# Zero rows as tasks of the sync queue, row numbers loaded per query block, and a new order, in a block-sparse attention with an MLP on one Trainium2 core

## The chip, the cores and the metric

One core of a Trainium2 chip runs the whole program: TensorE (PE), VectorE (DVE), ScalarE (ACT), GpSimd (POOL), the sync engine (SP) that only issues transfers here, and 16 DMA engines. The metric is device microseconds of one execution. The kernel before takes 737.58 us, the median of 3 runs (735.38 to 740.02).

## The reference

`q`, `k`, `v` have 4 batches, 8 heads, 768 positions and 64 columns. Positions fall into 24 blocks of 32. A query block sees its own and the two neighbouring key blocks, the first and the last block, and three sampled ones; the first and the last query block see all keys.

```python
    scores = scale * np.matmul(q, k.transpose(0, 1, 3, 2))
    mask = np.abs(blk_i - blk_j) <= window
    mask = mask | (blk_i == 0) | (blk_j == 0) | (blk_i == n_blocks - 1) | (blk_j == n_blocks - 1)
    for qb in range(n_blocks):
        for kb in sampled_blocks[qb]:
            mask[qb * block:(qb + 1) * block, kb * block:(kb + 1) * block] = True
    ...
    return np.matmul(attn, v)
    ...
    h = x @ w_in                      # 3072 x 512 by 512 x 2048
    g = h * np.tanh(softplus(h))
    return g @ w_out                  # 2048 x 512
```

## The kernel before, in words

**Attention.** Each batch is 13 jobs (52 in all): the two full query blocks alone, the other 22 in pairs. A job is: scores `s` on TensorE, row maximum `mx` (DVE) and its scaled form `nb`, exponentials `pt` (ACT), a transpose of the probabilities, the product `o` with the values, division `xs` and a 32 x 32 transpose `tx` (DVE), and the split of the result into two f16 parts `xh` and `xl`. Batch 0 works in f32 and transposes on TensorE (`t`, then a copy `pp`); batches 1 to 3 work in f16 pairs and transpose by a DMA of the sync queue (`pp_dma`, L880). There is one scores buffer in PSUM, so the scores of a job wait for the exponentials of the job before it.

**Keys and values of a pair.** `gather_k` copies three sampled key blocks into the buffer `kg` (POOL, or ACT when the planner likes that better); `gather_v` issues four or five DMAs on the sync queue from a copy of the values in DRAM, `vd`, into `vg`. Where a sampled block is already in the window or is sampled twice, the row number points at 32 **zero rows** behind the values of `vd`. `which` works out the row numbers (`offk`, `offv`) from the sampled blocks with some twenty small DVE instructions, clears a piece of SBUF and stores it as the zero rows of the four batches, four DMAs on ACT's queue (L400). The row numbers come into an engine's registers by `values_load` in `blocks_at` (TENSOR_LOAD, L663): six numbers at a time, those of both blocks of a pair, once for each engine that gathers for the pair.

**The MLP.** `w_in` comes in 8 pieces of 1 MB (`wr`, three buffers), `w_out` in 16 (`wor`). They are float64 in pairs of int32: DVE decodes them (L1040, L1043, L1046), a gram product on TensorE and two small steps give a scale, and ACT, POOL and DVE split them into two f16 parts `wi` and `wo`. For each of 12 tiles of 256 positions: 16 units of `h` (12 products each, L1184), the activation `g` on ACT, DVE and POOL, and 16 units of `y` (6 products each, L1244). The first `h` needs the result of jobs 0 to 4 and the first piece of `wi`.

**What sets the order.** The kernel writes all its tasks into a planner (`Plan`) that runs when the program is built. It keeps an estimated time for each engine, takes the task that can start first, and breaks ties by the numbers of `PRIO`. `START` holds an earliest time for the scores of the first 18 jobs, and `RES` how much MLP work is to be left when the last scores start. Each engine gets its instructions in the order in which they were taken and waits in that order. Where the planner expects TensorE idle in the first 150 us, `emit` puts products of zeros there (L1019). Each DMA takes the next of eight completion semaphores, in the order of the program, so a DMA waits until the one eight places ahead of it has landed.

Of the kernel before, what the change touches and what calls it, by code (L numbers as in the profile page):

```python
# [10 lines left out]
F16 = mybir.dt.float16  # L11
# [19 lines left out]
PRIO = {  # L31
    "zeros": (-1475,),
    "load32 k": (-845.8,),
    "load32 q": (-521.8, -448.8, -133.8),
    "load v": (-335.4, -495, -187.9, 230.7),
    "which": (-366.4,),
    "globals": (-1100, -6.6, -629.2, -149.6),
# [16 lines left out]
    "gsc": (-489.7,),  # L54
    "open": (507.5,),
    "s": (-363.8, 257.2, 138.7, 739),
    "mx": (-244, -319.1, 454.4, -635.3),
    "nb": (91.8, 609.2, 401.3, -77.9),
    "ex": (879.3, 387.6, 575.9, -27.9),
    "t": (-67.7, 16),  # L60
    "pp": (-8.1,),
    "o": (249.5, -772.8, 56.2, 280.6),
    "xs": (164.1, 687.9, 486.7, -162.2),
    "tx": (-80.3, 357.3, -117, -301.3),
    "xh": (795.7, -92.6, 151.3, -180.3),
    "xl": (-108.8, -149.4, -464.4, 487.1),
    "gather k": (-91.6, -283.6, -211.3, -794.3),
    "gather v": (-465, -812.9, -151.1, -1036),
    "load wo": (-701.2, -485, -180.9, 187.3),
    "decode wor": (338.6, 334.9, 656.5, 297.7),  # L70
    "gram y": (620.2,),
    "diag y": (-604.3,),
    "rootp wo": (-372.6,),
    "root wo": (-947.3,),
    "wo t": (112.9, -511.6, 53.8, 551.6),
    "wo hi": (-369.6, -312.8, -250.1, -464.2),
    "wo lo": (129.2, -136.8, -300.6, -232.5),
    "load k": (59, 59, 59, -132.3),
    "ss k": (70, 70, 70, 131),
    "sc k": (4, 356.4, -47.2, -105.6),  # L80
    "rootp k": (60, -634.9, -788.4, -43.6),
    "root k": (7, -763, -202.2, 176.7),
    "hi k": (52, 298, 502.1, 134.5),
    "lo k": (-79, -308.4, -18.8, -82.9),
    "load q": (59, 59, 59, 922.3),
    "ss q": (70, 70, 70, -319.9),
    "rootp q": (60, 231.2, 189.5, 65.7),
    "root q": (7, -0.7, 482.1, -278.2),
    "hi q": (52, -617.7, -813.9, -431.7),
    "lo q": (-79, -301.9, -459.2, 220.5),  # L90
    "clear": (-871.6,),
    "dense v": (-524.8, -820.3, -116.4, -411.5),
    "sc v": (4, -451.1, 413.1, -242.8),
    "ends": (13, 1272, 408.6, 260.5),
    "hi v": (52, 429.3, 414.7, 163.6),
    "lo v": (-79, -46.1, -130.6, -361.2),
    "hsc": (-629.6, -765.4, -588.2, 494.6),
    "osc": (-86, 750, 394.5, 691.1),
    "h16": (17, -34.8, 37, -408.3),
    "l16": (-40, -538.2, -718.8, -730.1),  # L100
    "tdma": (-60, 514.2, -156.5, 135.9),
    "xc": (1, 324.4, -257.5, 928.6),
    "kw": (8, -141.1, 764, 224.6),
    "hs": (268.3, -203.1, 55.1, 458.3),
    "us": (-570.1, -103.3, -302.2, -862.9),
    "us1": (240.2, -236.2, 174.8, 321.8),
    "us2": (515.7, 236.1, -874.1, -128.7),
    "ln": (-41.8, 181.7, -203.2, -276.7),
    "un": (353.1, 608.6, 449.1, 52.3),
    "hm": (-273.3, -620.2, 41, -1033),  # L110
    "gh": (-571.7, 417.5, -81.6, 428.6),
    "gl": (-58.7, 25.1, -179.3, -85.7),
    "ys": (-505.2, -22.3, -674.9, -34.6),
    "out": (577.4, 504.7, -100.7, -419.3),
# [21 lines left out]
class Plan:  # L136
# [47 lines left out]
    def emit(self, pace):  # L184
# [16 lines left out]
        while todo:  # L201
# [34 lines left out]
            if t.eng == "PE" and self.zeros and self.FROM < start < self.TILL and idle > 0.25:  # L236
                self.zeros(int(idle / 0.22))
            for e in t.ways:
# [43 lines left out]
def attn_mish_kernel(ctx: ExitStack, tc: tile.TileContext, qT, kT, v, sampled, blocks, w_in, w_out, out):  # L282
# [74 lines left out]
    def which(new):  # L357
        room = new(sb, "raw", ("z",), [P, RAW])
        at = [H * VW // 2]
# [28 lines left out]
        for r in range(1, NR):  # L388
            for r2 in range(r):
# [284 lines left out]
    def gather_k(su):  # L674
# [3 lines left out]
        def fn(eng):  # L678
            for j, c0 in zip(blocks_at(mybir.EngineType.Pool if eng == "POOL" else mybir.EngineType.Activation,
# [5 lines left out]
                else:  # L685
                    nc.scalar.activation(out=dst, in_=src, func=AF.Copy)  # L686
        add("POOL", 0.75 if exact(b) else 1.05, lambda: fn("POOL"), r=KT3(b) + ["off"], w=[("kg", n)], use=[("kt", b)], port=2, key=K("gather k", b),
            also=[("ACT", 0.65 if exact(b) else 0.95, lambda: fn("ACT"))])
        if su["whole"]:
            add("DVE", 0.44, lambda: nc.vector.tensor_copy(  # L690
                out=kgs[n][:, :, 0:WK], in_=tl["kt", b][:, :, (qb - 1) * BS:(qb + 2) * BS]),
                r=KT3(b), w=[("kw", n)], use=[("kt", b)], port=True, key=K("kw", b))

    def gather_v(su):
# [6 lines left out]
        def fn():  # L701
# [59 lines left out]
    def attend(job):  # L761
# [121 lines left out]
        for j in range(nt):  # L883
            kj, kpp, kp16 = ("t", i, j), ("pp", i, j), ("p16", i, j)
            if exact(b):
# [95 lines left out]
        add("DVE", 0.45 if nsu > 1 else 0.3, tx_fn, r=[("xs", i)], w=[("tx", i)], new=[("tx", ("tx", i))], key=K("tx", b))  # L981

# [19 lines left out]
        def xl_fn(eng):  # L1002
            run(lambda x, hi, lo: (nc.vector if eng == "DVE" else nc.gpsimd).tensor_tensor(out=lo, in0=x, in1=hi, op=ALU.subtract))  # L1003
# [459 lines left out]
```

## Time and profile before

| | us |
|---|---|
| median of 3 runs | 737.58 (735.38 to 740.02) |
| profiled execution, device time | 731.8 |
| its span, first to last instruction | 729.7 |
| around the span | 2.1 |
| TensorE busy | 687.9, of which products of zeros 39.1 |
| DVE, ACT, POOL busy | 565.8, 546.9, 241.7 |

Busy time says how long an engine worked, not what it waited for. Loading registers and issuing DMAs is not counted as busy, so that an engine of the profile can look idle while its sequencer is held. TensorE's busy time has work that produces nothing in it, the products of zeros.

### The profile page before, as it was taken

How to read it: one execution, taken by the hardware profiler on the slowest of the kernel's cores; microseconds unless marked ns; L12 is line 12 of the kernel's file. 1: busy time of each engine (PE TensorE's matmuls, PEld its weight loads, DVE VectorE, ACT ScalarE, POOL GpSimd, SP SyncE). 2: the span in 40 equal slices, each digit the busy share in tenths (PEclk: the TensorE clock that was granted, in tenths of full speed). 3: DMA queues.
4: the chain of work that ended last, by engine and by line, in shares of the span. 5: the costliest groups of instructions: out<-in, count | busy, mean ns of one | idle time of the engine just before them, and what ended most of it. 6: DMA issues, size and time to landing. Idle time of an engine off the chain costs nothing.

```text
span 729.7 us, 25410 instructions
## 1 busy us (share of the span) xinstructions
PE 687.9 (94%) x10383; PEld 452.4 (62%) x10383; DVE 565.8 (78%) x1065; ACT 546.9 (75%) x908; POOL 241.7 (33%) x314
## 2 busy tenths in 40 slices
PE   9888888898899899899999999999999999999997
PEld 3545576774466666565666666666666667666653
DVE  3788789899988878999888887979889878454350
ACT  2666666999888877898978889988898976464550
POOL 2266432276424423331423223543536521100000
PEclk9999999999999999999999999999999999999999
DMA  7978698432767877857798986795786666500000
GB/s 264 362 215 245 209 281 223 133 84 86 195 125 172 163 181 200 183 132 225 137 189 139 210 195 138 188 213 132 148 170 149 150 129 169 133 15 15 15 16 30
DMA packets 144600, 115.95 MB, mean 159 GB/s; under 512 B 96739, under 2 KB 107492, under 8 KB 144484
## 3 DMA queue, kind: packets, MB, share of 16 engines
q1 hardware_dynamic: 144288, 114.06, 62.9%
q8 instruction: 82, 1.34, 0.8%
q14 instruction: 34, 0.28, 0.1%
q10 hardware_dynamic: 196, 0.27, 0.1%
HBM read 79.32 MB, written 12.95 MB: 126 GB/s over the span
## 4 chain that ended last, share of the span: by engine, by line
PE 41%; DVE 16%; ACT 15%; DMA 13%; issue 7%; POOL 4%; SPq 2%; ACTq 2%; POOLq 1%; DVEq 0%
PE y L1244 18%; PE h L1184 16%; DMA raw_q<-in_q_dram 4%; ACT pt L825 3%; DMA pp<-p 2%; DMA wr<-in_moe_w_in_dram 2%; PE o L926 2%; DVE mx L799 2%; PE s L756 2%; ACT us L1215 2%; ACT us L1216 2%; DVE p L876 2%; DMA wor<-in_moe_w_out_dram 2%; ACTq L663 1%; DVE hs L1217 1%
## 5 line engine op out<-in xcount | busy, mean ns | idle before, releaser
L1184 PE MATMUL h<-xh,wi 128*128 128x256 f16 x1536 | 284.0, 274 | 1.3 <-POOL xh L1000 1.1
L1244 PE MATMUL y<-wo,g 128*128 128x512 f16 x1152 | 277.9, 380 | 4.6 <-ACT ys L1255 2.9
L1184 PEld LDWEIGHTS <-wi 128*128 128x128 f16 x2304 | 222.0, 98 | 60.4 <-issue 8.4
L1184 PE MATMUL h<-xl,wi 128*128 128x256 f16 x768 | 209.9, 273 | 0.9 <-POOL xl L1003 0.9
L1244 PEld LDWEIGHTS <-g 128*128 128x128 f16 x1152 | 109.7, 98 | 110.9 <-issue 11.4
L684 POOL COPY kg<-kt 128x256 f16 (+1 forms) x138 | 69.4, 542 | 149.4 <-PE s L756 110.2
L825 ACT ACTIVATE pt<-s,nb,ns 128x256 f32<-128x256 f32 (+1 forms) x208 | 106.6, 578 | 5.9 <-DVE nb L814 5.1
L1193 ACT ACTIVATE hs<-h,gsc 128x512 f32<-128x512 f32 x96 | 65.1, 678 | 44.8 <-PE h L1184 44.8
L1217 DVE SCALAR_TENSOR_TENSOR hs<-us,hs 128x1024 f32<-128x1024 f32 x48 | 59.9, 1249 | 23.5 <-ACT us L1216 23.2
L876 DVE SCALAR_TENSOR_TENSOR p<-pt,p 128x512 f16<-128x512 f32 (+1 forms) x102 | 65.5, 665 | 5.8 <-ACT p L869 5.1
L686 ACT ACTIVATE kg<-kt 128x256 f16 (+1 forms) x126 | 38.6, 373 | 30.6 <-DVE v L628 9.8
L799 DVE TENSOR_REDUCE mx<-s 128x4 f32<-128x1024 f32 x44 | 53.4, 1213 | 10.1 <-PE s L756 7.2
L1000 POOL CAST xh<-tx 128x256 f16<-128x256 f32 (+1 forms) x35 | 22.8, 659 | 114.0 <-DVE tx L980 102.4
L1211 DVE TENSOR_SCALAR us<-us 128x1024 f32<-128x1024 f32 x48 | 35.0, 729 | 30.1 <-ACT us L1207 29.7
L1003 POOL TENSOR_TENSOR xl<-tx,xh 128x256 f16<-128x256 f32 (+1 forms) x53 | 43.0, 816 | 42.1 <-ACT xh L998 23.5
L1207 ACT ACTIVATE us<-hs,hsc 128x1024 f32<-128x1024 f32 x48 | 55.1, 1148 | 1.0
L1215 ACT ACTIVATE us<-us 128x1024 f32<-128x1024 f32 x48 | 50.6, 1055 | 5.5 <-POOL us L1213 4.7
L1214 ACT ACTIVATE us<-us 128x1024 f32<-128x1024 f32 x37 | 39.1, 1056 | 18.4 <-DVE us L1211 18.3
L1216 ACT ACTIVATE us<-us 128x1024 f32<-128x1024 f32 x48 | 50.5, 1054 | 0.8
L1228 POOL TENSOR_TENSOR g<-hs,g 128x1024 f16<-128x1024 f32 x16 | 38.0, 2375 | 34.5 <-DVE g L1225 18.7
L1019 PE MATMUL zeros<-z 128*128 128x512 f16 x153 | 39.1, 402 | 3.7 <-issue 2.1
L926 PEld LDWEIGHTS <-pp 128*32 128x32 f16 x2952 | 32.6, 97 | 13.7 <-issue 11.4
(205 smaller groups left out, 908.7 us busy)
## 6 DMA issues: line engine op xcount, KB each, us to landing
vg<-vd SPq DMA_DIRECT2D x304, 65.0 KB, 2.3
vg<-vd SPq DMA_DIRECT2D x80, 195.0 KB, 3.1
wr<-in_moe_w_in_dram SPq DMA_DIRECT2D x8, 1024.0 KB, 9.2
wor<-in_moe_w_out_dram SPq DMA_DIRECT2D x16, 512.0 KB, 5.2
vd<-v SPq DMA_DIRECT2D x12, 520.0 KB, 5.0
raw_v<-in_v_dram SPq DMA_DIRECT2D x12, 512.0 KB, 6.1
out_dram<-ys SPq DMA_DIRECT2D x24, 256.0 KB, 2.3
raw_k<-in_k_dram SPq DMA_DIRECT2D x9, 512.0 KB, 5.9
```

What stands on the lines that cost most here:

```text
L684: nc.gpsimd.tensor_copy(out=dst, in_=src)
L799: nc.vector.tensor_reduce(out=mx.rearrange("p g w -> p (g w)"), in_=tl[ks].rearrange("p g (w k) -> p (g w) k", k=KT), axis=AX.X, op=ALU.max)
L825: ex = lambda o, x, g, w: nc.scalar.activation(out=o, in_=x, func=AF.Exp, bias=nb[:, g, w:w + 1], scale=ns(w)[:, 0:1])
L876: nc.vector.scalar_tensor_tensor(out=x[:, 1, cs], in0=src, scalar=PSC, in1=x[:, 0, cs], op0=ALU.mult, op1=ALU.subtract)
L926: nc.tensor.matmul(o[cs, at] if v1 == VW else o[cs, at, 0:v1 - v0], p[:, k, g, cs], x, start=j == 0 and g == 0 and k == 0 and n == 0, stop ...
L1184: nc.tensor.matmul(h[:, f2].rearrange("p (s q) -> p s q", q=BS), wi[:, fp, w, cc, fs], x[:, :, cc], start=f2 == 0 and k == 0, stop=f2 == 1 ...
L1193: nc.scalar.activation(out=tl[kq][:, 2 * (fp % 2):2 * (fp % 2) + 2], in_=tl[kh], func=AF.Copy, scale=gsc[:, fp:fp + 1])
L1207: nc.scalar.activation(out=new(sb, "us", ku, [P, 4, TT]), in_=hs(), func=AF.Exp, scale=hsc[:, b:b + 1])
L1215: add("ACT", 0.97, lambda: nc.scalar.activation(out=us(), in_=us(), func=AF.Ln, bias=1.0), w=[ku], key=K("ln", b))
L1216: add("ACT", 0.97, lambda: nc.scalar.activation(out=us(), in_=us(), func=AF.Exp, scale=-1.0), w=[ku], key=K("un", b))
L1217: add("DVE", 1.15, lambda: nc.vector.scalar_tensor_tensor(out=hs(), in0=us(), scalar=-0.5, in1=hs(), op0=ALU.add, op1=ALU.mult), r=[ku], w ...
L1244: nc.tensor.matmul(tl[ky], tl["g", b, t, k][:, g, f, q], wo[:, fc, w], start=fc == 0 and n == 0, stop=fc == NFC - 1 and n == 2)
```

## The change

- `which` no longer stores the zero rows. The cleared piece stays as `tl["z"]`, in a buffer of the ring `hs` in place of `raw`, and a task `zrow` for each batch stores it from the sync queue. `gather_v` of a batch waits for its own batch's zero rows.
- `su["first"]` is the query block itself and `n = NR`: three row numbers are loaded for each query block, on the engine that gathers for it.
- The number of products of zeros for an idle stretch is `(idle - 0.3) / 0.25` (0.4 in the first 15 us) in place of `idle / 0.22`: 105 are left of 153.
- Some of the planner's durations are other ones, and all of `PRIO`, `RES` and `START`, so that the order is another one on every engine.

```diff
 PRIO = {
-    "zeros": (-1475,),
...
+    "zrow": (-213.9, 259.7, 665, 36.4),
+    "zeros": (-1718,),
...
@@ emit
-                self.zeros(int(idle / 0.22))
+                self.zeros(int((idle - 0.3) / (0.25 if start > 15.0 else 0.4)))
@@ which
-        room = new(sb, "raw", ("z",), [P, RAW])
+        room = new(sb, "hs", ("z",), [P, 4, TT]).rearrange("p c t -> p (c t)")
...
-        z = room[0:BS, 0:H * VW // 2]
-        nc.gpsimd.memset(z, 0.0)
-        for b in range(B):
-            nc.scalar.dma_start(out=vd[b][S:S + BS].rearrange("s h d -> s (h d)"), in_=z if exact(b) else z.bitcast(F16))
+        tl["z"] = room[0:BS, 0:H * VW // 2]
+        nc.gpsimd.memset(tl["z"], 0.0)
+
+    def zrow(b):
+        nc.sync.dma_start(out=vd[b][S:S + BS].rearrange("s h d -> s (h d)"), in_=tl["z"] if exact(b) else tl["z"].bitcast(F16))
@@ blocks_at
-            n = 2 * NR
+            n = NR
@@ planner's durations
-        add("POOL", 0.75 if exact(b) else 1.05, lambda: fn("POOL"), ...
-            also=[("ACT", 0.65 if exact(b) else 0.95, lambda: fn("ACT"))])
+        add("POOL", 1.0 if exact(b) else 1.3, lambda: fn("POOL"), ...
+            also=[("ACT", 0.85 if exact(b) else 1.15, lambda: fn("ACT"))])
-        add("SP", 2.7, fn, r=VD3(b) + ["off", "z"], w=[("vg", n)], ...
+        add("SP", 3.1, fn, r=VD3(b) + ["off", ("z", b)], w=[("vg", n)], ...
-            add("SP", 0.3, lambda j=j: pp_dma(j), ...
+            add("SP", 1.35, lambda j=j: pp_dma(j), ...
-        add("DVE", 0.45 if nsu > 1 else 0.3, tx_fn, ...
+        add("DVE", 0.6 if nsu > 1 else 0.4, tx_fn, ...
@@ jobs
-            su["first"] = job["sus"][0]["qb"]
+            su["first"] = su["qb"]
@@ tasks
+    for b in range(B):
+        add("SP", 0.45, lambda b=b: zrow(b), r=["z"], w=[("z", b)], use=[("z",)], key=K("zrow", b), lat=2.2, kind=("dma", 0.4, 1))
@@ pace
-    RES, START = 142.9, [0, 2.2, 0.9, 28.4, 939.4, 56.8, 14.9, 34.5, 18.6, 102, ...
+    RES, START = 134.7, [5.3, 0, 0, 8.3, 31.4, 57, 38.1, 69.3, 35.4, 462.6, ...
```

The sync queue at the start of the program, before (`kt` and `q` are keys and queries of batch 0, `raw_v` its values, `wr` pieces of `w_in`, `vd` the values in DRAM):

```order
L512 DMA kt_0_123<-in_k_dram 128x4x768
L512 DMA q_0_0_157<-in_q_dram 128x4x256
L530 DMA raw_v_0_1_161<-in_v_dram 128x2x512
L512 DMA q_0_1_163<-in_q_dram 128x4x256
L530 DMA raw_v_0_0_165<-in_v_dram 128x2x512
L530 DMA raw_v_0_2_167<-in_v_dram 128x2x512
L1032 DMA wr_0_169<-in_moe_w_in_dram 128x4x512
L1032 DMA wr_1_171<-in_moe_w_in_dram 128x4x512
L1032 DMA wr_2_173<-in_moe_w_in_dram 128x4x512
```

The same place in the changed kernel:

```order
L514 DMA q_0_1_123<-in_q_dram 128x4x256
L514 DMA q_0_0_153<-in_q_dram 128x4x256
L514 DMA kt_0_157<-in_k_dram 128x4x768
L532 DMA raw_v_0_1_159<-in_v_dram 128x2x512
L532 DMA raw_v_0_0_161<-in_v_dram 128x2x512
L1034 DMA wr_0_163<-in_moe_w_in_dram 128x4x512
L532 DMA raw_v_0_2_165<-in_v_dram 128x2x512
L1034 DMA wr_1_167<-in_moe_w_in_dram 128x4x512
L402 DMA vd0_60<-z_125 32x520
L402 DMA vd3_63<-z_125 32x1040
L402 DMA vd1_61<-z_125 32x1040
L1034 DMA wr_2_215<-in_moe_w_in_dram 128x4x512
```

The first piece of `w_in` stands one place earlier, and the four zero stores, which stood on ACT's queue ahead of two of the value loads, stand behind the second piece.

VectorE around the scale of the last pieces of `w_in` (`gsc`), before (`xs_4`, `tx_4`: the result of job 4; `mx_7`: the maximum of job 7's scores; `wor`: pieces of `w_out`):

```order
L1154 TENSOR_SCALAR gsc_76<-iv_i_73,rg_1421 128x8
L1159 TENSOR_SCALAR hsc_81<-gmx_77,iv_x_78 128x1
L1043 SCALAR_TENSOR_TENSOR wo_72<-wor_4_1219,wo_72 128x512
L1046 SCALAR_TENSOR_TENSOR wo_72<-wor_1_1166,wo_72 128x512
L1040 TENSOR_SCALAR wo_72<-wor_5_1261 128x512
L947 TENSOR_SCALAR r_4_1473<-o_4_1238,iv_r_114 128x4
L951 RECIPROCAL r_4_1473<-r_4_1473 128x4
L962 TENSOR_TENSOR xs_4_1476<-o_4_1238,r_4_1473 128x256
L980 STREAM_TRANSPOSE tx_4_1518<-xs_4_1476 128x256
L799 TENSOR_REDUCE mx_7_1544<-s_7_1483 128x4
```

The same place in the changed kernel:

```order
L949 TENSOR_SCALAR r_4_1405<-o_4_1319,iv_r_114 128x4
L953 RECIPROCAL r_4_1405<-r_4_1405 128x4
L964 TENSOR_TENSOR xs_4_1408<-o_4_1319,r_4_1405 128x256
L1153 TENSOR_REDUCE gmx_77<-iv_i_73 128x1
L1155 RECIPROCAL rg_1430<-gmx_77 128x1
L1156 TENSOR_SCALAR gsc_76<-iv_i_73,rg_1430 128x8
L982 STREAM_TRANSPOSE tx_4_1466<-xs_4_1408 128x256
L1161 TENSOR_SCALAR hsc_81<-gmx_77,iv_x_78 128x1
L1045 SCALAR_TENSOR_TENSOR wo_72<-wor_3_1109,wo_72 128x512
L801 TENSOR_REDUCE mx_8_1491<-s_8_1433 128x4
```

Job 4's result, for which the first `h` waits, now stands ahead of the scale; the attention is one job further on, and the decoding of `w_out` less far.

TensorE at the last job's product `o_51`, before (only the first product of each unit is shown; a unit of `h` is 12, of `y` 6 products):

```order
L926 MATMUL o_51_14574<-vg1_112,pp_51_1_14268 32x65
...
L1244 MATMUL y_3_0_0_14315<-wo_72,g_3_0_3_14338 128x512
...
L1184 MATMUL h_3_1_4_14560<-xh_3_1_12706,wi_71 128x256
...
L1244 MATMUL y_3_0_1_14681<-wo_72,g_3_0_0_13996 128x512
...
L1184 MATMUL h_3_1_7_14783<-xh_3_1_12706,wi_71 128x256
...
L1184 MATMUL h_3_2_0_14826<-xh_3_2_13793,wi_71 128x256
```

The same place in the changed kernel:

```order
L928 MATMUL o_51_14309<-vg1_112,pp_51_1_14084 32x65
...
L1246 MATMUL y_3_0_1_14087<-wo_72,g_3_0_2_13558 128x512
...
L1186 MATMUL h_3_1_7_14296<-xh_3_1_12417,wi_71 128x256
...
L1246 MATMUL y_3_0_1_14087<-wo_72,g_3_0_3_13783 128x512
...
L1186 MATMUL h_3_2_0_14431<-xh_3_2_13538,wi_71 128x256
```

`h_3_2_0` is the first unit that needs job 51's result. Between the two stood 7 units of `h` and 8 of `y`; now there are one unit of `h` and three of `y`.

## Rows read from the trace of the kernel before

**Rows 1.** The page: the span; the chain that ended last, shares by engine (q: queue).

```profile
span 729.7 us, 25410 instructions
...
PE 41%; DVE 16%; ACT 15%; DMA 13%; issue 7%; POOL 4%; SPq 2%; ACTq 2%; POOLq 1%; DVEq 0%
```

**Rows 2.** Busy time by stage: length, engines (instructions), granted clock, DMA share, GB/s.

```profile
0.00:86.00 86.00, 72.34 (x1163) 40.85 (x1163) 63.12 (x126) 45.24 (x100) 37.85 (x50) 0.98 0.84 268
86.00:180.00 94.00, 84.94 (x1361) 63.92 (x1360) 82.87 (x153) 80.35 (x130) 43.79 (x53) 0.98 0.56 162
180.00:637.00 457.00, 441.90 (x7247) 292.80 (x7247) 386.30 (x747) 381.01 (x636) 158.92 (x211) 1.00 0.74 166
637.00:729.70 92.70, 88.71 (x627) 54.82 (x625) 33.52 (x41) 40.31 (x44) 1.11 (x1) 0.99 0.05 20
```

**Rows 3.** Busy time by stage, the products of zeros alone.

```profile
0.00:22.00 22.00, 18.18 (x69) 1.00 0.81 276
22.00:86.00 64.00, 20.54 (x83) 0.97 0.85 266
```

**Rows 4.** Timeline, TensorE: start, length, instruction [idle before, releaser].

```profile
1.69 11.11 PE L1019 MATMUL zeros<-z 128*128 128x512 f16 x37 [1.69 <-POOL z L1014]
12.73 1.52 PE L746 MATMUL s<-kt,q 64*32 64x512 f32 x32
...
86.00 0.36 PE L1184 MATMUL h<-xh,wi 128*128 128x256 f16 x1
```

**Rows 5.** Timeline of the queues of SP and ACT at the start.

```profile
7.59 6.75 SPq L530 DMA_DIRECT2D raw_v<-in_v_dram  x2
14.38 2.12 SPq L1032 DMA_DIRECT2D wr<-in_moe_w_in_dram  x3
...
26.48 4.73 SPq L1032 DMA_DIRECT2D wr<-in_moe_w_in_dram  x2
...
2.12 7.60 ACTq L400 DMA_DIRECT2D vd<-z  x4
```

**Rows 6.** Waits of the SP queue in 0 to 85 us: total, times, longest.

```profile
SPq L530 <- DMA vd<-z: 5.8, 1, 5.8
```

**Rows 7.** Timeline of VectorE at the start, the rows with idle time.

```profile
13.92 1.22 DVE L794 TENSOR_REDUCE mx<-s 128x2 f32<-128x1024 f32 x1 [2.48 <-PE s L746]
18.80 0.69 DVE L628 COPY v<-raw_v 128x1024 f32<-128x1024 f32 x1 [2.79 <-DMA raw_v<-in_v_dram]
22.23 0.69 DVE L1040 TENSOR_SCALAR wi<-wr 128x1024 int32<-128x1024 int32 x1 [2.74 <-DMA wr<-in_moe_w_in_dram]
```

**Rows 8.** Stretches of 20 us: TensorE, weight loads, DVE, ACT, POOL, clock, DMA.

```profile
0.00:20.00 20.00, 18.31 (x96) 7.35 (x97) 7.25 (x26) 5.95 (x12) 4.32 (x20) 1.00 0.79 269
20.00:40.00 20.00, 16.78 (x369) 11.36 (x368) 16.90 (x31) 13.34 (x30) 6.58 (x10) 1.00 1.01 344
```

**Rows 9.** The register loads of L663: count, duration ns min/median/max.

```profile
L663 SPq TENSOR_LOAD <-offv x44: 1263/1287/2710, 38.7 to 631.0; - x44
L663 POOLq TENSOR_LOAD <-offk x40: 1384/1424/3845, 7.6 to 586.0; - x40
L663 ACTq TENSOR_LOAD <-offk x38: 1321/1340/2771, 9.8 to 587.0; - x38
```

**Rows 10.** Timeline of TensorE from the last product of job 17 on.

```profile
244.74 0.91 PE L926 MATMUL o<-vg,pp 128*32 128x130 f16 x72
...
246.90 2.75 PE L1244 MATMUL y<-wo,g 128*128 128x512 f16 x12
250.79 0.27 PE L1184 MATMUL h<-xh,wi 128*128 128x256 f16 x1 [1.14 <-POOL xh L1000]
251.98 0.27 PE L1184 MATMUL h<-xl,wi 128*128 128x256 f16 x1 [0.92 <-POOL xl L1003]
```

**Rows 11.** Stretch of 20 us in which the granted clock fell (busy as in Rows 8).

```profile
100.00:120.00 20.00, 15.81 (x293) 0.91 0.86 243
```

**Rows 12.** The chain that ended last, in order of time: start, length, what.

```profile
617.16 1.29 PE y L1244 x6
618.45 1.31 PE h L1184 x12
```

More of the change, by code (lines that the diff above doesn't have):

```diff
@@ L31 @@
 PRIO = {
-    "zeros": (-1475,),
[L33 to L37, printed above, removed]
[16 rows of a table removed]
[L54 to L114, printed above, removed]
+    "zrow": (-213.9, 259.7, 665, 36.4),
@@ new lines @@
+    "zeros": (-1718,),
+    "load32 k": (-569.8,),
+    "load32 q": (-1080, -1105, -424.5),
+    "load v": (-308.3, -553.9, -18.4, 228.4),
+    "which": (293.9,),
+    "globals": (-1228, 199.5, -247.4, -581),
[16 rows of a table added]
+    "gsc": (-607.1,),
+    "open": (-76.5,),
+    "s": (-409.1, 152.1, 108.2, 1222),
+    "mx": (-192.9, -116.3, 558, -737.8),
+    "nb": (-173, 184.7, 451.3, 75),
+    "ex": (1355, 949.8, 866.2, 15.7),
+    "t": (-296.9, 16),
+    "pp": (62.8,),
+    "o": (318.8, 65.4, 471.5, 1186),
+    "xs": (-395.6, 599.7, 200.1, -548),
@@ new lines @@
+    "tx": (-2.6, 818.3, 148.1, -217.5),
+    "xh": (488.7, -363, 417.1, 9.1),
+    "xl": (-98.7, -498.7, -144.1, 574.7),
+    "gather k": (54, -532.1, -163.5, -722.2),
+    "gather v": (-528.2, -1015, -274.5, -1387),
+    "load wo": (-874.1, -495.8, 142, 465.5),
+    "decode wor": (592.8, 637.8, 1204, 992.1),
+    "gram y": (996.8,),
+    "diag y": (-528.8,),
+    "rootp wo": (-606.3,),
+    "root wo": (-1285,),
+    "wo t": (202.8, -716.5, -290.7, 581.7),
+    "wo hi": (-166.3, -241.9, -156.5, -1085),
@@ new lines @@
+    "wo lo": (233.1, -277.9, 40.9, -613.2),
+    "load k": (59, 59, 59, -33.4),
+    "ss k": (70, 70, 70, 974.8),
+    "sc k": (4, 1375, 843.5, 344.3),
+    "rootp k": (60, -73.2, -529.4, 489.9),
+    "root k": (7, -571.5, -753.3, -308.7),
+    "hi k": (52, 113.1, -736.9, 59.8),
+    "lo k": (-79, -11.1, -187.5, -231.2),
+    "load q": (59, 59, 59, 603.1),
+    "ss q": (70, 70, 70, -746),
+    "rootp q": (60, -19.3, 614.5, 522.8),
+    "root q": (7, 650.9, 1473, -248.3),
+    "hi q": (52, 333.2, -295.2, 534.9),
@@ new lines @@
+    "lo q": (-79, 475.3, -118.3, 449.3),
+    "clear": (-922.2,),
+    "dense v": (-909, -1036, -456.1, -65.5),
+    "sc v": (4, -209.1, 619.8, -652.8),
+    "ends": (13, 1051, -333.2, -241.3),
+    "hi v": (52, -50.8, -18.3, -575.4),
+    "lo v": (-79, -21.7, -118.2, -56.5),
+    "hsc": (-1282, -1484, -1153, 469),
+    "osc": (-185.3, 712.5, -85.1, 452.5),
+    "h16": (17, -199.4, -502.7, -99.1),
+    "l16": (-40, -304.5, -519.8, -284.6),
+    "tdma": (-60, 467.4, -13, 158.5),
+    "xc": (1, 201.8, -21.5, 1018),
@@ L115 @@
+    "kw": (8, 396.6, 874.8, 1111),
+    "hs": (676.2, -49.4, 146.5, 518.9),
+    "us": (-657.4, 294.4, -69.3, -1263),
+    "us1": (675.5, 56.1, 372.7, 619.9),
+    "us2": (1215, 32.1, -702.9, 166.3),
+    "ln": (-21.1, -271.8, -868.4, -662.2),
+    "un": (1243, 1374, 518.6, 600.6),
+    "hm": (-1280, -347, 137.2, -1278),
+    "gh": (-245.1, 889.2, 710.8, 904.9),
+    "gl": (702, -154.7, -270.5, -727.5),
+    "ys": (-210.1, 373.6, -724.5, 123.7),
+    "out": (419.7, 1262, -104.7, 543.3),
 }
@@ L686, in fn @@
                     nc.scalar.activation(out=dst, in_=src, func=AF.Copy)
-        add("POOL", 0.75 if exact(b) else 1.05, lambda: fn("POOL"), r=KT3(b) + ["off"], w=[("kg", n)], use=[("kt", b)], port=2, key=K("gather k", b),
-            also=[("ACT", 0.65 if exact(b) else 0.95, lambda: fn("ACT"))])
+        add("POOL", 1.0 if exact(b) else 1.3, lambda: fn("POOL"), r=KT3(b) + ["off"], w=[("kg", n)], use=[("kt", b)], port=2, key=K("gather k", b),
+            also=[("ACT", 0.85 if exact(b) else 1.15, lambda: fn("ACT"))])
         if su["whole"]:
-            add("DVE", 0.44, lambda: nc.vector.tensor_copy(
+            add("DVE", 0.3, lambda: nc.vector.tensor_copy(
                 out=kgs[n][:, :, 0:WK], in_=tl["kt", b][:, :, (qb - 1) * BS:(qb + 2) * BS]),
@@ L709, in fn @@
                 nc.sync.dma_start(out=vg[p0:p0 + BS, c0 // P], in_=vd[b][ds(j, BS)])
-        add("SP", 2.7, fn, r=VD3(b) + ["off", "z"], w=[("vg", n)], key=K("gather v", b), lat=1.8, kind=("dma", 1.1, NR + 1 + (a0 > 0) + (a1 < WK)))
+        add("SP", 3.1, fn, r=VD3(b) + ["off", ("z", b)], w=[("vg", n)], key=K("gather v", b), lat=1.8, kind=("dma", 1.1, NR + 1 + (a0 > 0) + (a1 < WK)))
     def fetch_dense(su):
@@ L894, in attend @@
             add("DVE", 0.75 if dense else 0.6, lambda j=j: l16_fn(j), r=[*ps_, ("h16", i, j)], w=[("l16", i, j)], use=[kp16, *kps], key=K("l16", b), port=True)
-            add("SP", 0.3, lambda j=j: pp_dma(j), r=[("h16", i, j), ("l16", i, j)], w=[("ph", i, j), ("pl", i, j)], use=[kpp, kp16],
+            add("SP", 1.35, lambda j=j: pp_dma(j), r=[("h16", i, j), ("l16", i, j)], w=[("ph", i, j), ("pl", i, j)], use=[kpp, kp16],
                 new=[("pp", kpp)], key=K("tdma", b), lat=1.8, kind=("dma", 1.75, 1))
@@ L980, in tx_fn @@
             nc.vector.transpose(tx if nsu > 1 else tx[:, 0], xs if nsu > 1 else xs[:, 0])
-        add("DVE", 0.45 if nsu > 1 else 0.3, tx_fn, r=[("xs", i)], w=[("tx", i)], new=[("tx", ("tx", i))], key=K("tx", b))
+        add("DVE", 0.6 if nsu > 1 else 0.4, tx_fn, r=[("xs", i)], w=[("tx", i)], new=[("tx", ("tx", i))], key=K("tx", b))
         fresh = [t for t in qts if ("x", b, t) not in xt]
@@ L1008, in attend @@
             also=[("POOL", (0.4, 0.65)[n], lambda: xh_fn("POOL")), ("DVE", (0.2, 0.28)[n], lambda: xh_fn("DVE"))])
-        add("POOL", (0.5, 0.75)[n], lambda: xl_fn("POOL"), r=[("tx", i), ("xhw", i)], w=[("xw", i)], use=kx, key=K("xl", b),
+        add("POOL", (0.5, 0.82)[n], lambda: xl_fn("POOL"), r=[("tx", i), ("xhw", i)], w=[("xw", i)], use=kx, key=K("xl", b),
             port=True, also=[("DVE", (0.3, 0.4)[n], lambda: xl_fn("DVE"))])
@@ L1302, in attn_mish_kernel @@
     add("ACT", 1.0, lambda: which(new), w=["off", "z"],
-        new=[("raw", ("z",))], key=K("which", 0), lat=6.0)
+        new=[("hs", ("z",))], key=K("which", 0), lat=5.2, kind=("dma", 0.0, 2))
+    for b in range(B):
+        add("SP", 0.45, lambda b=b: zrow(b), r=["z"], w=[("z", b)], use=[("z",)], key=K("zrow", b), lat=2.2, kind=("dma", 0.4, 1))
     globals_(0)
@@ L1386, in attn_mish_kernel @@
     total = sum(t.ways["PE"][0] for t in plan.tasks if t.kind and t.kind[0] == "M")
-    RES, START = 142.9, [0, 2.2, 0.9, 28.4, 939.4, 56.8, 14.9, 34.5, 18.6, 102, 75.8, 71.8, 144.1, 1792, 50.5, 27.1, 193.2, 56.8]
+    RES, START = 134.7, [5.3, 0, 0, 8.3, 31.4, 57, 38.1, 69.3, 35.4, 462.6, 14.5, 85.2, 61.4, 209.7, 97.2, 182, 105.2, 48.7]
     at = {"done": 0.0, "next": 0.0, "job": 0, "last": None, "shape": None}
```

32 rows, old and new, of the table PRIO are left out of this document.

## The prediction

> **What bounds the kernel now.** I read the busy time by stage first. From 86 us on TensorE is the bound: it is busy 84.9 of 94, 441.9 of 457 and 88.7 of 92.7 us, so that only 9.1, 15.1 and 4.0 us are idle [rows 2]. The stage before is another one: TensorE looks busy 72.3 of 86 us, but 18.2 + 20.5 = 38.7 of that are products of zeros [rows 3], so useful work fills 33.6 us and 52 are lost. Next the timeline of TensorE: the first scores start at 12.73 us, straight behind 37 products of zeros, and the first unit of the MLP at 86.00 [rows 4]. The MLP is what keeps TensorE full, so a microsecond by which its first unit comes earlier is worth a microsecond at the end, if the other engines can follow.
>
> What holds the front is read from VectorE's timeline and the queues. VectorE is busy 16.9 of the 20 us from 20 to 40 but 7.25 of the first 20 [rows 8]: it sat waiting for the scores (2.48), a piece of the values (2.79) and the first piece of `w_in` (2.74), which it decodes only at 22.23 [rows 7]. That piece was issued at 14.38, behind two loads of values that held the sync queue from 7.59 on [rows 5], and one of these waited 5.8 us for a zero row to land [rows 6]: the four zero stores, 7.6 us long on ACT's queue [rows 5], take four of the eight completion semaphores, and a load eight places on waits for them. The fourth and fifth pieces come at 26.48 [rows 5], when the first piece is decoded and its buffer is free. So the zero rows push the whole stream of `w_in` back. The chain of waits says the same more roughly: TensorE has 41% of it, VectorE 16%, DMA 13% [rows 1].
>
> **The change, part by part.** The sum is made against the profiled execution: span 729.7, device time 731.8, which is 5.8 below the median of 737.58.
>
> *Zero rows and order at the start.* The first piece of `w_in` is now the sixth DMA of the sync queue and needs no earlier one landed among the eight semaphores. Ahead of its end stand 1.5 MB of keys, 1 MB of queries, 1 MB of values and its own 1 MB, 4.5 in all; at the 344 GB/s that the stretch from 20 to 40 reached [rows 8] that is 13 us after the first issue, so about 14.5 to 16 us in place of 22.2. The zero stores (65 KB each) wait in the sync queue behind the second piece; the stores of `vd` and the third piece wait behind them, yet those came at 16.6 and later before. Of VectorE's three waits (8.0 us) I take 6 as gone: the scores come sooner too (14 fewer products of zeros ahead of them, 11.11 / 37 = 0.30 us each [rows 4], of which some 2.5 us can be used before keys and queries have landed). In both orders VectorE has about the same work ahead of the scale of the last pieces, and job 4's result, for which the first `h` waits, stands ahead of that scale now. I add 2 us for this. So the first `h` comes 8 us earlier, near 78. Lower bound: nothing, if the DMAs, at a share of 1.01 from 20 to 40 us [rows 8], bring the later pieces no sooner. Upper bound 12: the three waits, and half of the 8 us by which the zero stores and the first piece moved.
>
> *Fewer products of zeros.* 48 fewer; the 34 behind the first scores, at 20.54 / 83 = 0.25 us [rows 3], free 8.4 us that TensorE would otherwise wait. Nothing, unless they had delayed something: 0 to -2.
>
> *Row numbers.* Before, six numbers took 1.34 us on ACT (38 times), 1.42 on POOL (40) and 1.29 on SP (44) [rows 9]; now three numbers, 43, 45 and 88 times. No row shows a load of three. Between the full price and half of it, ACT and POOL together go from 108 us to between 121 and 61, SP from 57 to between 113 and 57. With nothing nearer than the row itself I take the middle, about 1 us: SP +28, ACT and POOL -17. The queues of SP, ACT and POOL had 2, 2 and 1% of the chain, 36 us with all they do [rows 1], and TensorE's idle time from 180 to 637 is 15.1 [rows 2], so little of either reaches the end: 0, between -5 and +8. The Trainium skill (Runtime: NRT & Kernel Launch, Instruction fetch mechanics) puts such a load at some 200 ns a register: six are 1.2 us, which the trace's 1.29 bears out, and three would be an estimated 0.6; by that SP would pay nothing more, ACT and POOL save some 47 us, and the term would be -3.
>
> *Shorter cover between attention and MLP.* Before the first unit of a tile, TensorE needs other work while the last job's result is divided, transposed and split. At the last product of job 17 that took from about 245.6 to 251.98, 6.4 us, with 4.1 us of work in between, and TensorE waited 1.14 + 0.92 [rows 10]. In the new order the work in between is 3.5, 6.1, 5.2 and 5.2 us at tiles 0 of batches 1 to 3 and the last tile (one unit of `h` and three of `y`); before it was 3.9, 12.2, 17.0 and 19.5 (counted in the two orders with 1.31 us a unit of `h`, 1.29 of `y` [rows 12]). At 6.4 us the new waits sum to 0.4 + 0.3 + 1.2 + 1.2 = 3. I take +2; 0 to +5.
>
> *The rest of the order.* The last job's product now stands 17 units of `h` and 34 of `y` before the end (66 us) in place of 23 and 41 (83 us), so the attention of batches 1 to 3 is spread over more time, and VectorE, busy 386 of 457 us there [rows 2], gets some air. The planner's new durations are nearer to what the queues take. Against that stand new places for waits that no row can show. I take -2.5 of the 24 us idle between 86 and 637, with -10 and +10 as ends.
>
> Sum: -8 + 0 + 0 + 2 - 2.5 = -8.5: span 721.2, and 729 against the median.
>
> **The rivals.**
> *The front gains, VectorE takes it back (0.20).* From 86 to 180 us VectorE is busy 82.9 and ACT 80.4 of 94 [rows 2]; they have the same work there. If 8 us less are left for it, TensorE waits for them, and the time is about 737, no change. Against it: VectorE's 11 us idle there could be used.
> *The waits go as well (0.13).* The front's upper bound, 12, and half of the 15 idle us from 180 to 637: some 718.
> *Slower: the sync queue (0.08).* If a load of three costs the full 1.29 us, the second gather of each of the 33 pairs of batches 1 to 3 issues its last DMAs 1.29 us later, 42 us in all on a queue that works in order, with the transposing DMAs of the probabilities behind it, and `o` waits for both. It outweighs the gain when more than 8.5 of the 42 reach TensorE; with half of them the time is 729 + 21 = 750. For it: the row has one price whatever the engine. Against it: SP's share of the chain is 2% [rows 1].
> *The clock (0.04).* With fewer products of zeros the granted clock may fall in the front. It read 0.91 in one stretch without them [rows 11], which is a fall to 1.2 GHz for part of it. If a quarter of the front's 33.6 us of useful work ran at half clock, it would take 8 us more: 737. The Trainium skill (TensorE: Matmul & The Clock Gate, What's actually happening) has the slow clock as the resting state, from which activity releases the array; the 0.91 agrees, and by that rule the change's fewer products speak against it.
>
> **How the numbers follow.** The forecast has 0.55, from 722 to 736. About 1% (7.4 us) is what a measurement of this kernel can tell from no change. Below 730.2 lie two thirds of the forecast and the second rival: 0.50 faster. The rest of the forecast, the first rival and the clock: 0.41 the same. Slower, 0.09: the sync queue and a little of the rest's upper end. The range from 717 to 742 takes in the forecast with its bounds, the first rival and most of the second.
>
> **What would show it.** The first decode of `wr` at 15 to 17 us in place of 22.23, the first scores near 10.5, the first `h` at 76 to 80, with TensorE's idle time from there on no more than the 28 us of before: then the front is right. TensorE or VectorE rows that wait between 80 and 170 us for each other would be the first rival. The median of L663 tells the price of a load at once; waits of `o` for `vg` or `pp` by the sync queue would be the slower rival. Waits of the first `h` of a tile for `xh` and `xl` are the cover. I am wrong if the first `h` does not move.

## The result, and the profile after

The changed kernel takes 720.63 us, the median of 4 runs (718.97 to 720.83), against 738.62 for the kernel before (735.38 to 740.02, 4 runs): ratio 0.9758, 95% interval 0.972 to 0.9795. In a second measurement, beside experiments below, it took 721.12 against 735.75: 0.9798 (0.9761 to 0.9835). So 15 to 18 us less, where 8.5 were forecast; the direction and the range (717 to 742) held, the size did not, and both medians lie just under the forecast's own 722 to 736. Ratios are of usual executions alone, and some medians of the kernel before take in a few slower ones, so differences from it are given by the ratio.

Of the page: the span, and the chain by engine, as in [rows 1]. The span fell by 12.5 us, less than the medians, because the profiled execution of before was a fast one. The mean granted clock in it was 0.992; 17 timed runs of before had 0.987 in the mean. Half a per cent of 735 us is an estimated 3.7 of the 5.8 by which that profile lay below its median.

```profile
span 717.2 us, 25362 instructions
...
PE 47%; DVE 20%; ACT 16%; DMA 8%; issue 5%; POOL 2%; ACTq 0%; POOLq 0%; SPq 0%; DVEq 0%
```

The three queues, 5% of the chain together before, are gone from it. Busy time by stage, as in [rows 2] (length, engines, granted clock, DMA share, GB/s):

```profile
0.00:80.00 80.00, 63.56 (x1146) 37.15 (x1147) 61.09 (x124) 45.70 (x100) 34.92 (x57) 0.96 0.87 279
80.00:180.00 100.00, 88.64 (x1382) 65.67 (x1381) 87.74 (x161) 85.92 (x132) 44.10 (x50) 0.97 0.58 170
180.00:637.00 457.00, 447.10 (x7273) 298.58 (x7272) 390.95 (x777) 376.22 (x628) 142.39 (x188) 1.00 0.72 164
637.00:717.20 80.20, 76.21 (x540) 46.22 (x538) 28.63 (x36) 36.27 (x40) 2.56 (x2) 1.00 0.07 24
```

From 180 to 637 us TensorE idles 9.9 us in place of 15.1. From the first `h` on it idles 11.4 + 9.9 + 4.0 = 25.3 us, within the 28 that the prediction named. From 80 to 180 us, though, there is a long wait that before has not: TensorE stands still for 4.60 us until ACT, busy splitting `w_out`, has read a unit of `h` (`hs`). The clock read 0.50 from 154 to 160 us behind it, which is 1.2 GHz. All nine profiles in this order have this wait (4.60 to 4.69 us) and the slow clock behind it:

```profile
155.26 0.37 PE L1186 MATMUL h<-xh,wi 128*128 128x256 f16 x1 [4.60 <-ACT hs L1195]
```

At the start, the timelines of TensorE, VectorE and the sync queue, answering [rows 4, 5, 7]:

```profile
10.37 1.52 PE L748 MATMUL s<-kt,q 64*32 64x512 f32 x32 [0.97 <-DMA kt<-in_k_dram]
...
79.66 0.27 PE L1186 MATMUL h<-xh,wi 128*128 128x256 f16 x1
```
```profile
15.68 0.69 DVE L1042 TENSOR_SCALAR wi<-wr 128x1024 int32<-128x1024 int32 x1 [1.03 <-DMA wr<-in_moe_w_in_dram]
```
```profile
3.67 0.68 SPq L1034 DMA_DIRECT2D wr<-in_moe_w_in_dram  x1
4.86 1.75 SPq L532 DMA_DIRECT2D raw_v<-in_v_dram  x1
6.66 1.32 SPq L1034 DMA_DIRECT2D wr<-in_moe_w_in_dram  x1
8.09 3.46 SPq L402 DMA_DIRECT2D vd<-z  x3
```

The first piece of `w_in` is issued at 3.67 us (14.38 before) and decoded at 15.68 (22.23), the first scores start at 10.37 (12.73), the first `h` at 79.66 (86.00). The register loads (count, duration ns min/median/max), answering [rows 9]: half the price for half the numbers.

```profile
L665 SPq TENSOR_LOAD <-offv x88: 663/676/1713, 32.0 to 638.3; - x88
L665 POOLq TENSOR_LOAD <-offk x45: 722/732/1993, 10.3 to 564.4; - x45
L665 ACTq TENSOR_LOAD <-offk x43: 687/705/1807, 5.4 to 588.0; - x43
```

By count times median, ACT's loads fall from 51 to 30 us and POOL's from 57 to 33; SP's stay (57 and 59).

### The profile page after: what moved, and what is told of

It is laid out like the page before. It is cut to its first block, busy times and chain, and to the rows that moved or that the text cites. A ratio compares the mean times of both kernels' runs of the same rounds, so it can differ in the third digit from the quotient of the medians.

```text
span 717.2 us, 25362 instructions
## 1 busy us (share of the span) xinstructions
PE 675.5 (94%) x10335; PEld 447.6 (62%) x10335; DVE 568.4 (79%) x1095; ACT 544.1 (76%) x897; POOL 224.0 (31%) x295
## 4 chain that ended last, share of the span: by engine, by line
PE 47%; DVE 20%; ACT 16%; DMA 8%; issue 5%; POOL 2%; ACTq 0%; POOLq 0%; SPq 0%; DVEq 0%
PE y L1246 21%; PE h L1186 19%; DMA wr<-in_moe_w_in_dram 3%; DVE p L878 3%; ACT pt L827 3%; PE o L928 3%; PE s L758 3%; DVE mx L801 2%; DMA vg<-vd 2%; ACT us L1217 2%; DVE hs L1219 2%; ACT us L1218 1%; ACT hs L1195 1%; DMA wor<-in_moe_w_out_dram 1%; DVE p L873 1%
## 5 line engine op out<-in xcount | busy, mean ns | idle before, releaser
L686 POOL COPY kg<-kt 128x256 f16 (+1 forms) x135 | 65.0, 519 | 135.2 <-PE s L758 110.3
L878 DVE SCALAR_TENSOR_TENSOR p<-pt,p 128x512 f16<-128x512 f32 (+1 forms) x102 | 67.4, 682 | 3.7 <-ACT p L871 3.3
L1002 POOL CAST xh<-tx 128x256 f16<-128x256 f32 (+1 forms) x32 | 20.5, 648 | 126.1 <-DVE tx L982 125.1
L688 ACT ACTIVATE kg<-kt 128x256 f16 (+1 forms) x129 | 40.4, 379 | 15.6 <-DMA kt<-in_k_dram 8.2
L1213 DVE TENSOR_SCALAR us<-us 128x1024 f32<-128x1024 f32 x48 | 33.5, 698 | 15.4 <-ACT us L1209 15.0
L1005 POOL TENSOR_TENSOR xl<-tx,xh 128x256 f16<-128x256 f32 (+1 forms) x39 | 32.5, 839 | 37.5 <-ACT xh L1000 28.4
L928 PEld LDWEIGHTS <-pp 128*32 128x32 f16 x2952 | 32.6, 97 | 11.8 <-issue 11.4
L1232 DVE TENSOR_TENSOR g<-hs,g 128x1024 f16<-128x1024 f32 x31 | 38.6, 1245 | 0.8 <-ACT g L1225 0.4
```

What stands on the lines that cost most here:

```text
L686: nc.gpsimd.tensor_copy(out=dst, in_=src)
L878: nc.vector.scalar_tensor_tensor(out=x[:, 1, cs], in0=src, scalar=PSC, in1=x[:, 0, cs], op0=ALU.mult, op1=ALU.subtract)
L928: nc.tensor.matmul(o[cs, at] if v1 == VW else o[cs, at, 0:v1 - v0], p[:, k, g, cs], x, start=j == 0 and g == 0 and k == 0 and n == 0, stop ...
```

## The experiments

Each ran in several rounds beside the kernel before on the same chip; ratios are to it. Except in the one with the old pacing, the instructions of TensorE and VectorE stand in the order of the kernel that was edited, products of zeros apart.

**Six numbers a load again.**

```diff
-            n = NR
+            n = 2 * NR
...
-            su["first"] = su["qb"]
+            su["first"] = job["sus"][0]["qb"]
```

> The changed kernel with six row numbers a load again, the order untouched: 44 loads on SP, some 78 on ACT and POOL. Theory A (the loads are worth time): ACT and POOL get some 45 us of loading back, kg comes later, and a tenth of it reaches TensorE: 724 to 727 us against 720.6. Theory B (what came after the first 13 scores is the order): 720 to 722, with the load's median back at 1.3 to 1.4 us.

Measured: 728.96 us, 0.9924 (0.9896 to 0.9952), some 8 us above the changed kernel, whose intervals lie below. Theory A, and more than it asked for. The loads were 83 on ACT and POOL, some 50 us more than in the changed kernel by count times median, and SP's took 56 us in place of 59, so the loss is put down to ACT and POOL. A part of where it goes is seen in one place. In the chain of waits of this run (start, length, what), ACT's loads stand ahead of the exponentials that free the scores buffer:

```profile
241.72 1.06 ACT us L1217
242.77 0.91 ACTq L665
...
244.15 0.70 ACT kg L688 x2
244.85 0.57 ACT hs L1195
245.42 0.06 ACT pt L827
245.48 0.06 issue
245.54 0.79 ACTq L665
246.33 0.64 ACT us L1209
246.97 0.29 issue
247.26 1.03 ACT pt L827 x2
248.29 0.04 issue
248.33 1.48 PE s L758 x42
```

TensorE's timeline, first in this run, then at the same instruction of the changed kernel:

```profile
248.33 1.48 PE L758 MATMUL s<-kg,q 64*32 64x256 f16 x48 [3.58 <-ACT pt L827]
```
```profile
243.31 0.85 PE L758 MATMUL s<-kg,q 64*32 64x256 f16 x48 [0.74 <-ACT pt L827]
```

The wait is 3.58 us in place of 0.74, and the same products take 1.48 us in place of 0.85: behind the wait the granted clock is at 0.50, which is 1.2 GHz, for some 3 us of the two stretches below that read 0.59 and 0.56. Stretches of 2 us of this run (TensorE busy, clock, DMA share, GB/s):

```profile
246.00:248.00 2.00, 0.00 (x0) 1.00 0.61 178
248.00:250.00 2.00, 1.67 (x50) 0.59 0.54 129
250.00:252.00 2.00, 2.00 (x12) 0.56 1.07 375
252.00:254.00 2.00, 2.00 (x15) 1.00 1.08 350
```

Together some 4.5 us at one place: 2.8 us of wait and an estimated 1.7 us of the clock. By 425 us the run is 9 us behind this profile of the changed kernel, and 5 behind another that is shown further down.

**The old number of products of zeros.**

```diff
-                self.zeros(int((idle - 0.3) / (0.25 if start > 15.0 else 0.4)))
+                self.zeros(int(idle / 0.22))
```

> The changed kernel with the old number of products of zeros (163 in place of 105), the order untouched. If the clock that fell to 0.87 from 40 to 60 us costs time: the clock is back at 1.00 there, the first unit of h comes 1 to 3 us earlier, 718 to 719.6 us. If the zeros delay what they precede: the first scores 1 to 2 us later, 721 to 723. If neither: 720.6 within 0.7.

Measured: 723.3 us, 0.9853 (0.9804 to 0.9902), not to be told from the changed kernel. The stretch from 40 to 60 us, of the changed kernel and then of this run:

```profile
40.00:60.00 20.00, 12.83 (x218) 7.50 (x226) 14.99 (x28) 9.16 (x15) 8.86 (x5) 0.87 0.72 204
```
```profile
40.00:60.00 20.00, 15.47 (x269) 9.11 (x267) 18.19 (x26) 10.06 (x19) 13.97 (x9) 1.00 0.82 215
```

The clock is back at 1.00, and still the first `h` came at 81.30, not earlier than 79.66. But the first scores came 3 us later than the changed kernel's 10.37, behind 44 products of zeros in place of 23, the sign of the second theory:

```profile
13.38 1.52 PE L748 MATMUL s<-kt,q 64*32 64x512 f32 x32
```

So this run alone can't separate the two. The order alone, further down, has both the old zeros and a clock of 1.00 up to 80 us, and its first `h` is at 79.06: no sign that the clock cost the front anything. The medians differ by 2.2 us and the intervals overlap, so that what fewer products are worth is not shown beyond that.

**The zero rows stored by ACT.**

```diff
+        for b in range(B):
+            nc.scalar.dma_start(out=vd[b][S:S + BS].rearrange("s h d -> s (h d)"), in_=tl["z"] if exact(b) else tl["z"].bitcast(F16))
     def zrow(b):
-        nc.sync.dma_start(out=vd[b][S:S + BS].rearrange("s h d -> s (h d)"), in_=tl["z"] if exact(b) else tl["z"].bitcast(F16))
+        pass
```

> The changed kernel with the four zero stores issued by ACT inside which, all else and the order untouched. Theory of the prediction (the zero stores hold a load eight places on and push w_in back): first decode of wr 3 to 6 us later than 15.68, first h 2 to 6 us later, 722 to 726 us. Rival (it is the place of the first piece in the sync queue, not the zero stores, that brought it forward): first decode within 1 us of 15.68, 720 to 721.5 us.

Measured: 721.47 us, 0.9824 (0.9771 to 0.9876): not to be told from the changed kernel. Waits of the sync queue in the first 40 us:

```profile
SPq L534 <- DMA kt<-in_k_dram: 3.8, 1, 3.8
...
SPq L534 <- DMA q<-in_q_dram: 1.9, 1, 1.9
```

The queue was held by loads eight places back again, yet the first piece was decoded at 16.22 and the first `h` came at 78.77. The rival's signs came. The piece was issued 4.5 us before the third load of values, and it is that load which waited 3.8 us for `kt` (sync queue's timeline, this run):

```profile
6.27 0.68 SPq L1036 DMA_DIRECT2D wr<-in_moe_w_in_dram  x1
...
10.80 0.37 SPq L534 DMA_DIRECT2D raw_v<-in_v_dram  x1
```

In the kernel before the piece stood behind that load, and the loads of values had waited for `kt` too, not only for a zero row (5.8 us [rows 6]):

```profile
SPq L530 <- DMA kt<-in_k_dram: 4.6, 1, 4.6
```

So in the new order the zero stores' queue is worth nothing that was measured. Moving them alone in the old order was not run, nor the piece's place alone; other loads moved in the new order as well.

**The order alone**: the three edits above, made together.

> The new order alone: six numbers a load, the old number of zeros and the zero stores on ACT, all three undone together. If the three parts are worth what the prediction gave them (0 for loads and zeros, some of the front's 8 for the zero rows): 721 to 726 us. If the loads are worth the half that the forecast lacked: 727 to 731. If the order is everything: 720 to 722.

Measured: 731.04 us, 0.9945 (0.9912 to 0.9978): some 4 us less than before. The first `h` is at 79.06, so the front's gain is the order's; but ACT's first activation of the 13th group of four `h` units starts at 265.7 us, behind before's 263.7 (that of the first group: 88.4 against 97.9). So 11.5 us are lost in between. The changed kernel loses 4.2 of them too (89.4 and 259.4), and both have the wait of 4.6 us for `hs` there. Of the rest, a part is at the place shown above: a wait of 3.35 us of `s` for `pt` and the slow clock behind it. This run has the loads of six too.

**The three-number loads in the kernel before.** The first experiment's edit the other way round, in the old order.

> The kernel before with three row numbers a load and nothing else changed, its order untouched. If the shorter loads are worth 8 us whatever the order: 727 to 731 us where before has 735 to 739. If they are worth that only in the new order, which leaves ACT less air: within 2 us of before (the prediction's term of 0). If the 44 more loads on SP cost: slower by 2 us or more.

Measured: 735.04 us, 1.0009 (0.9972 to 1.0046): nothing, within some 3 us. TensorE's waits from 180 to 640 us for gathered values in before, and in this run:

```profile
PE o L926 <- DMA vg<-vd: 1.3, 1, 1.3
```
```profile
PE o L926 <- DMA vg<-vd: 4.2, 4, 1.7
```

**The same on ACT and POOL alone, SP at six.**

```diff
-        qb = su["first"]
+        qb = su["first"] if eng == mybir.EngineType.SP else su["qb"]
...
-            n = 2 * NR
+            n = 2 * NR if eng == mybir.EngineType.SP else NR
```

> The kernel before, its order untouched, with three numbers a load on ACT and POOL alone; SP keeps its 44 loads of six. With three on SP as well nothing was gained, and o of batches 1 to 3 waited 4.2 us for vg in place of 1.3. If SP's 44 further loads ate what ACT and POOL gained (the prediction's slower rival at half its price): that wait back near 1.3 us, 728 to 733 us where before has 735 to 738. If the old order gains nothing from shorter loads on ACT and POOL: within 2 us of before.

Measured: 729.94 us, 0.9931 (0.9894 to 0.9968). So shorter loads on ACT and POOL are worth some 5 us (2 to 8) in the old order too, and by the difference of the two runs, which were on two chips, 44 further loads on SP ate them. The wait that was to show it does not: it was 5.4 us in this profile, not 1.3. That execution was one of the longest of the twelve (736.73), and where SP's loads cost stays open.

**Six numbers on one engine.** Three of each six are unused.

```diff
-            n = NR
+            n = NR * (2 if eng == mybir.EngineType.Activation else 1)
```

> The changed kernel with six numbers in each of ACT's 43 loads (three of them unused), SP and POOL at three: some 27 us more on ACT's queue. If ACT's queue is where the loads count (TensorE's scores wait for pt, which stands behind a load): 727 to 731 us, the whole of what six numbers everywhere took. If it is SP or POOL: within 2 us of the changed kernel.

Measured: 727.81 us, 0.9892 (0.9857 to 0.9928): 6.7 above the changed kernel run beside it. `s` waits for `pt` more than in the changed kernel's two profiles (TensorE's waits, 180 to 640 us; their rows behind it):

```profile
PE s L758 <- ACT pt L827: 4.5, 4, 1.7
```
```profile
PE s L758 <- ACT pt L827: 0.7, 1, 0.7
```
```profile
PE s L758 <- ACT pt L827: 1.4, 2, 1.0
```

With `EngineType.SP` in that line:

> The changed kernel with six numbers in each of SP's 88 loads (three of them unused), ACT and POOL at three: some 54 us more on SP's queue. This is the prediction's slower rival made true: 88 loads at the full price. That rival: 740 us or more. If SP's queue has room: within 3 us of the changed kernel.

Measured: 729.0 us, 0.9916 (0.9884 to 0.9949): 7.9 above, between the two expectations. In the same stretch `o` waits more for the gathered values, which is the place that the prediction's slower rival named (this run; then the changed kernel run beside it, whose other profile has no such wait):

```profile
PE o L928 <- DMA vg<-vd: 3.5, 5, 0.9
```
```profile
PE o L928 <- DMA vg<-vd: 0.5, 2, 0.4
```

The changed kernel that ran beside these:

> The changed kernel itself, as the base of the runs beside it: 720 to 723 us.

Measured: 721.12 us, as given above. Its profiled execution had a span of 723.2, 6.0 longer than the one shown above. Some 3 of that lie at the first `h` of a tile near 400 us. First the earlier profile, then this one (timeline; then stretches of 2 us):

```profile
400.35 0.27 PE L1186 MATMUL h<-xh,wi 128*128 128x256 f16 x1 [2.15 <-POOL xh L1002]
401.27 0.27 PE L1186 MATMUL h<-xl,wi 128*128 128x256 f16 x1 [0.66 <-POOL xl L1005]
```
```profile
402.08 0.37 PE L1186 MATMUL h<-xh,wi 128*128 128x256 f16 x1 [2.29 <-POOL xh L1002]
403.01 0.37 PE L1186 MATMUL h<-xl,wi 128*128 128x256 f16 x1 [0.55 <-POOL xl L1005]
```
```profile
402.00:404.00 2.00, 1.36 (x6) 0.50 1.06 371
404.00:406.00 2.00, 2.00 (x10) 0.50 1.11 326
406.00:408.00 2.00, 2.00 (x6) 0.50 1.21 227
408.00:410.00 2.00, 2.00 (x45) 0.84 0.12 45
```

The waits are nearly the same; but here the clock stays at 0.50 for some 7 us behind them, which loses some 3.4 us, and there it read 1.00.

**The row numbers kept in registers.** They are the same in all four batches, and here each engine keeps those of up to 16 query blocks.

```diff
+        if (eng, qb) in regs:
+            return regs[eng, qb]
         _, at = nc.values_load_multi_w_load_instructions(
...
+        if qb not in ONCE[eng]:
+            regs[eng, qb] = at
```

> The changed kernel, its order untouched, with row numbers kept in the registers: the numbers of a query block are the same in all four batches, and each engine keeps those of up to 16 blocks after the first load. Loads: SP 40 in place of 88, ACT 19 in place of 43, POOL 22 in place of 45, so 32, 17 and 17 us less on their queues. If the new order still waits for loads at the rate at which longer ones cost it (6.7 us for 27 on ACT, 7.9 for 54 on SP): 4 to 8 us less than the changed kernel, 713 to 717. If the loads of three were short enough to be hidden: 720 to 722.

Measured: 717.87 us (716.97 to 719.17), 0.9758 (0.9713 to 0.9803): the lowest median of all, some 3 us under the changed kernel's. But the ratio is the one that the changed kernel itself had in its first measurement, so a gain over it is not shown, and the time lies between the two expectations.

> The kernel before, its order untouched, with the row numbers kept in the same way: SP 40 loads of three in place of 44 of six, ACT 22 in place of 38, POOL 22 in place of 40; 30, 35 and 41 us less on the queues. If the old order doesn't wait for loads at all: within 2 us of before. If three numbers a load gave it nothing only because SP's second load came later: 728 to 732.

Measured: 723.35 us, 0.9815 (0.9764 to 0.9866): some 12 us under the old order with loads of three. Neither expectation: the old order did wait for loads. It gains 10 to 17 us over before, most of what the whole change gained. Compared with the run that left SP at six, SP has 30 us less of loads, ACT 14 and POOL 18; which of the three counts most was not separated.

**The old pacing.**

```diff
-    RES, START = 134.7, [5.3, 0, 0, 8.3, 31.4, ...]
+    RES, START = 142.9, [0, 2.2, 0.9, 28.4, 939.4, ...]
```

> The changed kernel with RES and START of before, so another order from the first jobs on, with the new priorities and the new loads. If the gain is the new code in any order that brings the first h forward: 720 to 726 us. If the order is a fit to its own numbers: 728 us or more. The first h says which part of the front the start times made (79.7 in the changed kernel, 86.0 before).

Measured: 743.42 us, 1.0082 (1.005 to 1.0114), with the first `h` at 112.54 us. The new priorities with the old `RES` and start times are over 20 us worse than the changed kernel, new code and all, so the order's numbers fit only each other. The first decode came at 15.6 us and the first scores at 10.3 here as well: an early first piece alone does not bring the first `h` forward.

## Why the prediction was right, and half the size

*The step that failed is the term of the row numbers*: "so little of either reaches the end: 0, between -5 and +8". In the new order it is -8, outside its own bounds. In the old order the same edit gave 0, so the worth depends on the order, which the term left out. Two more things were wrong in it. The price: 0.68 to 0.73 us a load, not the middle of 1 us. By the Trainium skill (Runtime: NRT & Kernel Launch, Instruction fetch mechanics), some 200 ns a register, it would have been an estimated 0.6, and the trace agrees within 0.13, though the page has such loads from HBM and the row numbers lie in SBUF. The term by it, -3, was on the right side and still too small; by its own figures ACT and POOL would save 108 - 88 x 0.6 = 55 us, not 47. And the reasoning: a share of 2% in the chain was taken as the worth of a queue. The chain shows one path. A load on ACT stands between other work and `pt`, and `s` waits behind; with six numbers everywhere one such wait was 3.6 us, with the slow clock behind it. At the end 27 us more of loads on ACT cost 6.7 us, and 52 more on SP 7.9.

*The front, -8.* The milestones came: decode at 15.68 (15 to 17 foretold), scores at 10.37 (10.5), first `h` at 79.66 (76 to 80), so -6.3. The cause given for it did not hold up: in the new order the zero stores on ACT's queue left all of it in place. It is the new order's; that it is the first piece's place in the sync queue is borne out by the waits, not by a run of its own.

*The zeros, 0 (0 to -2)*, agrees with the run that put them back. *The cover, +2*: the first `h` of later tiles waited 3.3 us in all (2.2 for `xh` on POOL, 0.9 for `xl`, 0.2 for `xh` on ACT) where before had 2.1 [rows 10], so +1.2 where +3 was worked out and +2 taken. The places were others: 2.8 of it at the tile near 400 us, where 0.3 was worked out. The clock behind it, 3.4 us in one of two profiles, was not thought of.

*The order*, front, cover and rest together, was forecast at -8.5 and measured alone, with loads of six, at about -4. A part of the front's gain is lost between 80 and 180 us, where TensorE waits 4.6 us for ACT and the clock falls behind it: the first rival's sign, with ACT in the place of VectorE. More is lost near 250 us, behind ACT's loads.

*The rivals.* The slower one, the sync queue, has a true mechanism: 44 more loads took about 5 us in the old order, and at full price 88 took 7.9 in the new, which would have left the change 6 us faster, not slower; its price of half of 42 us was too high. The clock fell to 0.87 in the front, with no sign of a cost there. "The waits go as well", 718, was the nearest, but by luck: the waits from 180 to 637 us did fall by a third, while the 12 us of its front did not come, and the loads' 8 made up for them.

The sum as measured, one part undone at a time: order -4, loads -8, zero rows 0, zeros 0 to -2, so -12 to -14, against -14 to -15 in the second measurement. In the first, with -18, the kernel before took 2.9 us more than in the second. Direction and range hold for the order alone too, so that they came true is not luck. The larger part of the size is the loads', which the forecast put at nothing.

## What to carry to other kernels

Register loads and DMA issues are in no engine's busy time: add count times median to the busy time of the engine whose queue they stand in before you call it idle, and don't take a queue's share of the chain for its worth. An edit and a new order can't be priced apart: the same shorter loads gave 0 in one order and 8 us in the other. Numbers that don't change between passes can stay in registers: against loads of three that gave some 12 us in the old order, and nothing that could be told from noise in the new one.

## What was not expected of the hardware

A register load of three numbers takes 0.68 us on SP, 0.71 on ACT and 0.73 on POOL, of six 1.28, 1.34 and 1.40: some 0.2 us a number. A wait of TensorE of 2.1 to 2.4 us in the middle of dense work, at the same place near 400 us in six profiles of the new order, was followed by 3 to 7 us at 1.2 GHz in three of them and by none in the other three. Where the 7 us followed, the wait cost more than twice its length. Behind the 4.6 us wait for `hs` the clock fell in all nine profiles. How much of the spread between runs of one kernel (717.53 to 725.04) this makes is not shown: two of these runs had a mean clock of 0.985 and 0.986, and took 725.04 and 719.10 us.
